# Decoding the weights of both layers inside the convolution stage, with operands in PSUM, and a three-pass filter transform

## The chip, the cores and the metric

One core of one Trainium2 chip runs the kernel. Its engines are TensorE (PE, matmuls; PEld is its weight load), VectorE (DVE), ScalarE (ACT), GpSimd (POOL) and the queues that issue DMAs (SP's and ACT's here). The metric is the device time of one execution in microseconds (us), the median of several.

## What is computed

A long convolution gates an input and is followed by two feed-forward layers. Cut to what matters:

```python
# x, v: (2, 12480, 128); filter from a small MLP times exp(-0.01 * pos)
h_filt = (np.maximum(pos_emb @ w1, 0.0) @ w2) * window
Uf = np.fft.rfft(x * v, n=2 * S, axis=1)
Hf = np.fft.rfft(h_filt, n=2 * S, axis=0)
y = np.fft.irfft(Uf * Hf[None], n=2 * S, axis=1)[:, :S]
a = (x * y).reshape(24960, 128)
h = a @ moe_w_in;  b = elu(h) @ moe_w_out           # 128 -> 2048 -> 128
h = b @ moe2_w_in; out = (h * np.cos(h)) @ moe2_w_out
```

The four weight matrices (128 x 2048 and 2048 x 128) reach the chip as 64-bit floats, so the kernel has to turn each into float32 with integer and float operations on its two 32-bit words. That is the decode. The layers multiply in fp32r, with each operand split into a high and a low part and three products in place of one float32 product, so the decode ends by splitting each weight into `hi` and `lo` too.

## The kernel before

**Stages.** The program is written by hand in one order for each engine: the engines take their instructions in the order of the Python code, and wait for each other by semaphores. A first stage (to some 50 us) makes the filter taps `h_all`. The second is the convolution, and then the two layers run over 52 tiles of 480 tokens each.

**The convolution** works on 32 groups of four channels (`NCH`, index `c`), in a software pipeline written as a table, `steps` (L424): each turn `p` of the loop at L427 runs each entry `(f, back, k)` for the group `p - back`. The stages are four small transforms. `st_a` (L330): PE multiplies by `fa_t` into `ps_a`, DVE makes `za` and `zb` by the twiddle factors, POOL adds them into `z_t`. `st_b` (L348): PE multiplies `z_t` by `dft_t` into `ps_b`. For `k == 2` this is the filter, and ACT copies the result to `hr` and `hi_f`. For `k` of 0 or 1 it is one of the two batches, and three DVE steps form the product with the filter (`ya`, `ps_b` in place, `y_t`); ACT rounds it to `yh`. `lo_y` (L326): POOL makes the rest `yl`. `st_c` (L376): PE transforms back into `ps_c`, in three fp32r passes, DVE makes `wa` and `wb`, POOL adds them into `w_t`. `st_d` (L401): PE makes `ps_d`, DVE multiplies by x into `at`, and SP's queue writes it to `xt_d` in DRAM. `prod` is POOL's product x * v (`u_t`), and `load` asks SP's queue for the next x and v. So a turn has three `st_a`, three `st_b`, two `st_c` and two `st_d`. `st_a` and `st_b` multiply in float32 (one such product is two PE instructions in the trace), `st_c` in fp32r.

**The decode of the first layer** is 16 jobs of 256 columns (`Decode`, L96). Between stages the loop takes one piece of it (`next(now)`, L432). On DVE it is `sg` and `mag` (sign and magnitude of the top word), `keep`, `bits`, `av` and `pw` (L119 to L141), all with operands in SBUF; on ACT `sq`, `lf` and `hi`; on POOL `bv`, `dv` and `lo`. SP's queue writes `hi` and `lo` to `w_d`.

**The layers.** Block `n` is a tile and one of eight groups of 256 hidden columns. `gemm1` (L496) makes `h_ps` with six fp32r matmuls of 480 columns; in layer 1, ACT's exponential and tanh and four DVE steps (L519, L521) make the activation; POOL or ACT and POOL split it (L93, L94); `gemm2` (L559) follows five blocks behind, with two of the eight groups in plain float32 (`gf`, eight PE instructions in a tile). After the last block of a tile ACT copies the result out (L578).

**The decode of the second layer** (`arena`, L592) is 8 jobs of 512 columns in free parts of `x1`. One piece of it stands behind each `gemm1` of the blocks 8 to 199 (L625). Here DVE does `dv` and `lo` as well (L161, L163, `self.e`).

Of the kernel before, what the change touches and what calls it, by code (L numbers as in the profile page):

```python
# [74 lines left out]
def hyena_moe_kernel(ctx: ExitStack, tc: tile.TileContext, x, v, pe, w1, w2,  # L75
# [20 lines left out]
    class Decode:  # L96


        def __init__(self, alloc, n, layer, which, q):
# [24 lines left out]

        def split(self):
            self.hi, self.lo = self.t("hi", F32R), self.t("lo", F32R)
            if not self.wide:
                self.av = self.raw
                copy_r(self.hi, self.raw)
                yield  # L130
                return
            keep, bits, self.av, pw, self.bv = (self.t("keep", I32), self.t("bits", I32), self.t("av", F32),
                                                self.t("pw", I32), self.t("bv", F32))
            nc.vector.tensor_scalar(keep, self.sq, TINY * TINY, -1.0, op0=ALU.is_ge, op1=ALU.mult)
            yield
            nc.vector.scalar_tensor_tensor(bits, self.mag, 0x40000000, self.sg,
                                           op0=ALU.bitwise_xor, op1=ALU.bitwise_or)
            yield
            nc.vector.tensor_tensor(self.av.bitcast(I32), bits, keep, op=ALU.bitwise_and)  # L139
            yield  # L140
            nc.vector.tensor_scalar(pw, self.av.bitcast(I32), -8388608, None, op0=ALU.bitwise_and)  # L141
            copy_r(self.hi, self.av)
            yield
            nc.gpsimd.tensor_tensor(self.bv, self.lf, pw.bitcast(F32), op=ALU.mult)
            yield

        def store(self):
            l, wh, n, p = self.layer, self.which, self.n, self.o
            nc.sync.dma_start(w_d[l, wh, 0, :, p:p + n], self.hi.bitcast(F32))
            for m in FULL[l] if wh else ():  # L150
                o = m * 256 - p
                if 0 <= o < n:
                    full = self.av[:, o:o + 256]
                    if self.wide:
                        full = self.t("full", F32)[:, 0:256]
                        nc.gpsimd.tensor_tensor(full, self.av[:, o:o + 256], self.bv[:, o:o + 256], op=ALU.add)
                        yield
                    nc.sync.dma_start(wf_d[l, m], full)
            if self.wide:
                dv = self.t("dv", F32)  # L160
                self.e.tensor_tensor(dv, self.av, self.hi.bitcast(F32), op=ALU.subtract)  # L161
                yield
                self.e.tensor_tensor(self.lo, dv, self.bv, op=ALU.add)  # L163
            else:
                nc.gpsimd.tensor_tensor(self.lo, self.av, self.hi.bitcast(F32), op=ALU.subtract)
            yield
            nc.sync.dma_start(w_d[l, wh, 1, :, p:p + n], self.lo.bitcast(F32))

        def run(self):
            for part in (self.words, self.split, self.store):  # L170
                yield from part()

    with tc.manual_schedule():
        with ExitStack() as cs:
# [132 lines left out]
            with ExitStack() as vs:  # L307
# [3 lines left out]
                pd = vs.enter_context(tc.tile_pool(name="pd", bufs=2, space=PSUM))  # L311
# [366 lines left out]
```

## Time and profile before

| | us |
|---|---|
| median of three runs | 3029.52 (3028.1 to 3030.63) |
| the profiled execution, its own time | 3032.04 |
| its span in the trace | 3030.2 |
| filter taps, first instruction to first `st_a` | 50.7 |
| convolution, first `st_a` to first `gemm1` | 689.5 |
| layer 1, first `gemm1` to its last copy-out (start) | 1169.5 |
| layer 2, from there to its last copy-out (start) | 1116.9 |

All stage times are differences of start times in the trace. The span is cut into these four by what PE does. Within a stage, the time from one occurrence of the same step to the next (one turn of the convolution's loop, one tile of a layer) tells more than the busy share of an engine over the span.

### The profile page before, as it was taken

The numbers are of one execution on the slowest core, as the hardware profiler recorded it, in microseconds if no ns is written. First come the engines' busy times: TensorE is split into PE (matmuls) and PEld (weight loads), VectorE is DVE, ScalarE is ACT, GpSimd is POOL, SyncE is SP. The second block draws the span as 40 slices with busy tenths as digits, with TensorE's granted clock in tenths as the row PEclk, the third lists the DMA queues.
The fourth block names the chain that finished last, engine by engine and source line by source line (L and its number), as shares of the span: only waits on it lengthen the run. The fifth ranks groups of instructions, "written<-read, shape, count | busy, mean of one in ns | idle before, by whom it ended". The sixth has DMA issues, their size and how long they took to land.

```text
span 3030.2 us, 38341 instructions
## 1 busy us (share of the span) xinstructions
PE 2966.4 (98%) x13140; PEld 2317.9 (76%) x13140; DVE 2587.9 (85%) x3272; ACT 2006.6 (66%) x3076; POOL 2575.1 (85%) x1632
## 2 busy tenths in 40 slices
PE   8999999998999999999999999999999999999999
PEld 6777677775777777888888887787888878888887
DVE  5999987876999998888888888788888888888887
ACT  2111111112887888888888888788888888888887
POOL 4888877775898998888888888888888888888888
PEclk9999999998999999999999999999999999999999
DMA  3232322222011100000000001000000000000000
GB/s 103 76 84 78 87 63 64 63 53 88 24 38 38 45 21 10 14 10 14 10 14 11 14 11 40 23 14 10 14 11 13 11 14 10 14 11 14 11 14 14
DMA packets 79635, 96.16 MB, mean 32 GB/s; under 512 B 5722, under 2 KB 63096, under 8 KB 79442
## 3 DMA queue, kind: packets, MB, share of 16 engines
q1 hardware_dynamic: 74016, 88.07, 10.0%
q10 hardware_dynamic: 5426, 5.65, 0.6%
q8 instruction: 105, 1.72, 0.2%
q14 instruction: 88, 0.72, 0.1%
HBM read 59.16 MB, written 34.54 MB: 31 GB/s over the span
## 4 chain that ended last, share of the span: by engine, by line
PE 83%; DVE 12%; issue 2%; ACT 2%; POOL 1%; DMA 0%; POOLq 0%; ACTq 0%; DVEq 0%
PE o_ps L573 34%; PE h_ps L504 32%; PE ps_b L356 6%; PE ps_c L387 4%; PE ps_d L405 2%; PE ps_a L336 2%; DVE e L519 2%; DVE e L521 2%; DVE wb L391 1%; DVE wa L391 1%; DVE ya L368 1%; DVE av L139 1%; ACT e L515 1%; DVE ps_b L369 1%; DVE zb L341 1%
## 5 line engine op out<-in xcount | busy, mean ns | idle before, releaser
L94 POOL TENSOR_TENSOR gl<-e,gh 128x960 fp32r<-128x960 f32 x624 | 1414.7, 2274 | 127.3 <-ACT gh L85 92.6
L504 PE MATMUL h_ps<-xh,w 128*128 128x480 f32 x3328 | 1074.8, 404 | 26.6 <-DVE e L521 22.6
L504 PEld LDWEIGHTS h_ps<-xh,w 128*128 128x128 f32 x3328 | 623.4, 188 | 220.6 <-issue 73.0
L573 PE MATMUL o_ps<-gh,w 128*128 128x480 f32 x2496 | 746.7, 380 | 0.0
L534 DVE SCALAR_TENSOR_TENSOR e<-e,h_ps 128x960 f32<-128x960 int32 x416 | 480.2, 1154 | 201.6 <-ACT e L532 146.9
L504 PE MATMUL h_ps<-xl,w 128*128 128x480 f32 x1664 | 632.8, 380 | 0.1
L519 DVE SCALAR_TENSOR_TENSOR e<-e,t_ps 128x480 f32<-128x480 f32 x832 | 534.4, 651 | 96.2 <-ACT t_ps L517 87.6
L515 ACT ACTIVATE e<-h_ps 128x480 f32<-128x480 f32 x832 | 473.0, 569 | 173.4 <-PE h_ps L504 143.7
L532 ACT ACTIVATE e<-h_ps 128x960 int32<-128x960 f32 x416 | 404.2, 972 | 200.0 <-PE h_ps L504 197.0
L573 PEld LDWEIGHTS o_ps<-gh,w 128*128 128x128 f32 x2496 | 468.9, 188 | 76.1 <-issue 0.8
L93 POOL TENSOR_SCALAR gh<-e 128x960 fp32r<-128x960 f32 x416 | 422.9, 1017 | 114.8 <-DVE e L521 88.9
L517 ACT ACTIVATE t_ps<-h_ps 128x480 f32<-128x480 f32 x832 | 476.4, 573 | 15.6 <-DVE e L519 15.5
L573 PE MATMUL o_ps<-gl,w 128*128 128x480 f32 x1248 | 476.4, 382 | 3.0 <-POOL gl L94 2.9
L541 ACT ACTIVATE e<-e,half_pi 128x960 f32<-128x960 f32 x416 | 453.6, 1090 | 0.3 <-DVE e L534 0.3
L521 DVE SCALAR_TENSOR_TENSOR e<-e,h_ps 128x480 f32<-128x480 f32 x624 | 377.6, 646 | 0.0
L573 PE MATMUL o_ps<-gf,wf 128*128 128x480 f32 x832 | 368.6, 565 | 0.0
L543 DVE TENSOR_TENSOR e<-e,h_ps 128x960 f32<-128x960 f32 x312 | 358.1, 1148 | 1.3 <-ACT e L541 1.2
L504 PEld LDWEIGHTS h_ps<-xl,w 128*128 128x128 f32 x1664 | 313.0, 188 | 53.3 <-POOL xl L94 0.8
L85 ACT ACTIVATE yh<-y_t 128x720 fp32r<-128x720 f32 x64 | 51.5, 805 | 411.2 <-DVE y_t L371 335.9
L573 PEld LDWEIGHTS o_ps<-gl,w 128*128 128x128 f32 x1248 | 234.7, 188 | 42.3 <-POOL gl L94 5.0
L356 PE MATMUL ps_b<-z_t,dft_t 128*128 128x360 f32 x768 | 254.3, 475 | 8.8 <-DVE y_t L371 8.2
L344 POOL TENSOR_TENSOR z_t<-za,zb 128x720 f32<-128x720 f32 x96 | 141.9, 1478 | 114.2 <-DVE zb L341 114.2
(94 smaller groups left out, 3479.0 us busy)
## 6 DMA issues: line engine op xcount, KB each, us to landing
x_t<-in_x SPq DMA_DIRECT2D x32, 392.0 KB
v_t<-in_v SPq DMA_DIRECT2D x32, 392.0 KB
xt_d<-at SPq DMA_DIRECT2D x64, 196.0 KB
out<-ot SPq DMA_DIRECT2D x52, 240.0 KB
x_in<-xt_d SPq DMA_DIRECT2D x50, 240.0 KB
w_d<-x SPq DMA_DIRECT2D x16, 256.0 KB
w<-w_d ACTq DMA_DIRECT2D x14, 256.0 KB
w<-w_d SPq DMA_DIRECT2D x14, 256.0 KB
```

Of the source, the lines that this page charges most:

```text
L93: ENG[plan[0]].tensor_scalar(hi, full, 1.0, 0.0, op0=ALU.mult, op1=ALU.add)
L94: ENG[plan[1]].tensor_tensor(lo, full, hi.bitcast(F32), op=ALU.subtract)
L356: nc.tensor.matmul(ps[:, r, 0:n], dft_t[:, sl], z[:, q], start=j == 0, stop=j == 1)
L504: nc.tensor.matmul(h[:, 0:T], a, b, start=k == 0, stop=k == 2)
L515: nc.scalar.activation(u[:, e], hs[e][:, 0:T], AF.Exp)
L517: nc.scalar.activation(ts[e][:, 0:T], hs[e][:, 0:T], AF.Tanh, scale=0.5)
L519: nc.vector.scalar_tensor_tensor(u[:, e], u[:, e], 1.0, ts[e][:, 0:T], op0=ALU.add, op1=ALU.mult)
L521: nc.vector.scalar_tensor_tensor(gt[:, e], u[:, e], 0.0, hs[e][:, 0:T], op0=ALU.min, op1=ALU.max)
L532: nc.scalar.activation(kq, hv, AF.Copy, scale=1.0 / TWO_PI, bias=0.25)
L534: nc.vector.scalar_tensor_tensor(rr, kq, -TWO_PI, hv, op0=ALU.mult, op1=ALU.add)
L541: nc.scalar.activation(rr, rr, AF.Sin, bias=half_pi)
L573: nc.tensor.matmul(o, a, b[:, e], start=f == 0 and k == 0, stop=f == NFT - 1 and k == len(mm) - 1)
```

## The change

All 32 jobs of both layers (256 columns each) are decoded in the convolution, and nothing of it is left in the layers. The decode is rewritten. ACT copies the top word into a PSUM tile `ps_w`, whose second half takes intermediate words, and does five more steps (`sq`, `keep` by Sign, `power`, `lf`, `hi`). DVE has four steps, `size`, `part`, `mag` and `pw`, each with at least one operand in `ps_w` and at most one in SBUF. POOL has three (`lf` times `pw`, `full`, `lo`). The pieces are taken by two generators, one for ACT's and DVE's part (`top`, four a turn) and one for POOL's (`low`, three a turn), which stand as entries in `steps`.

The filter's `st_b` (`k == 2`) becomes three fp32r passes, so `st_a` with `k == 2` gets a step of ACT (`zh`) and POOL one (`zl`, `lo_z`). `ps_d` has one bank in place of two, and the bank goes to `ps_w`. The table `steps` has another order: `st_b` of batch 0, `st_c` of batch 1 and `st_d` of batch 0 each come a turn later than before, and `load` comes at a turn's end.

```diff
+            sq, keep, power, size = self.t("sq", F32), self.t("keep", I32), self.t("power", I32), self.t("size", I32)
+            self.mag, self.lf, self.pw = self.t("mag", I32), self.t("lf", F32), self.t("pw", I32)
+            ps = bank.tile([128, 2, 256], F32, name="ps_w")
+            word, part = ps[:, 0].bitcast(I32), ps[:, 1].bitcast(I32)
+            nc.scalar.activation(ps[:, 0], top.bitcast(F32), AF.Copy)
+            nc.scalar.activation(sq, top.bitcast(F32), AF.Square)
             yield
+            nc.vector.tensor_scalar(size, word, 0x0FFFFFFF, 3, op0=ALU.bitwise_and, op1=ALU.logical_shift_left)
+            nc.scalar.activation(keep, sq, AF.Sign, scale=-1.0, bias=below)
+            yield
+            nc.vector.scalar_tensor_tensor(part, word, -2147483648, size, op0=ALU.bitwise_and, op1=ALU.bitwise_or)
+            nc.scalar.activation(power, keep, AF.Copy, scale=2.0 ** 23)
+            yield
+            nc.vector.scalar_tensor_tensor(self.mag, part, 0x40000000, keep, op0=ALU.bitwise_xor, op1=ALU.bitwise_and)
             nc.scalar.activation(self.lf, low.bitcast(U32), AF.Copy, scale=2.0 ** -52)
             yield
+            nc.vector.scalar_tensor_tensor(self.pw, part, 0x40000000, power, op0=ALU.bitwise_xor, op1=ALU.bitwise_and)
...
+                self.full = self.t("full", F32)
+                nc.gpsimd.tensor_tensor(self.lf, self.lf, self.pw.bitcast(F32), op=ALU.mult)
                 yield
+                nc.gpsimd.tensor_tensor(self.full, self.mag.bitcast(F32), self.lf, op=ALU.add)
+            hi, lo = self.t("hi", F32R), self.t("lo", F32R)
+            copy_r(hi, self.full)
             yield
+            nc.gpsimd.tensor_tensor(lo, self.full, hi.bitcast(F32), op=ALU.subtract)
+            nc.sync.dma_start(w_d[l, wh, 0, :, p:p + n], hi.bitcast(F32))
...
-                pd = vs.enter_context(tc.tile_pool(name="pd", bufs=2, space=PSUM))
+                pd = vs.enter_context(tc.tile_pool(name="pd", bufs=1, space=PSUM))
+                bank = vs.enter_context(tc.tile_pool(name="bank", bufs=1, space=PSUM))
...
+                    if k == 2:
+                        zh = p1.tile([NB, 2, DC * NF], F32R, name="zh")
+                        copy_r(zh, z)
+                        z = (z, zh)
                     zz[c, k] = z
+
+                def lo_z(c, k):
+                    z, zh = zz[c, k]
+                    zl = p1.tile([NB, 2, DC * NF], F32R, name="zl")
+                    nc.gpsimd.tensor_tensor(zl, z, zh.bitcast(F32), op=ALU.subtract)
+                    zz[c, k] = (zh, zl)
...
-                            nc.tensor.matmul(ps[:, r, 0:n], dft_t[:, sl], z[:, q], start=j == 0, stop=j == 1)
+                            if k == 2:
+                                zh, zl = z
+                                mm = ((dft_h, zh), (dft_l, zh), (dft_h, zl))
+                            else:
+                                mm = ((dft_t, z),)
...
-                steps = ((st_a, 0, 2), (st_b, 1, 1), (lo_y, 1, 0), (st_d, 2, 1), (prod, 0, 1), (st_a, 0, 0),
-                         (lo_y, 1, 1), (prod, -1, 0), (st_c, 1, 0), (st_b, 0, 2), (st_a, 0, 1),
-                         (st_c, 1, 1), (st_b, 0, 0), (st_d, 1, 0))
+                steps = ((st_b, 1, 0), (prod, 0, 1), (top, 0, 0), (lo_y, 1, 0), (low, 0, 0), (top, 0, 1), (st_a, 0, 2),
+                         (st_c, 2, 1), (top, 0, 2), (lo_z, 0, 2), (low, 0, 1), (st_b, 1, 1), (st_a, 0, 0), (lo_y, 1, 1),
+                         (st_d, 2, 0), (low, 0, 2), (st_c, 1, 0), (prod, -1, 0), (st_b, 0, 2), (st_a, 0, 1), (top, 0, 3),
+                         (st_d, 2, 1))
...
-        later = arena()
...
-                if 8 <= n < 200:
-                    next(later, None)
```

What POOL has in one turn of the convolution, before (one of the turns with decode; `bv`, `dv` and `lo` are its decode):

```order
L328 TENSOR_TENSOR yl_2319<-y_t_2276,yh_2278 128x720
L317 TENSOR_TENSOR u_t_2337<-x_t_1994,v_t_1995 98x512
L344 TENSOR_TENSOR z_t_2348<-za_2344,zb_2345 128x720
L328 TENSOR_TENSOR yl_2351<-y_t_2315,yh_2317 128x720
L317 TENSOR_TENSOR u_t_2354<-x_t_2175,v_t_2176 98x512
L398 TENSOR_TENSOR w_t_2389<-wa_2385,wb_2386 90x1024
L344 TENSOR_TENSOR z_t_2412<-za_2408,zb_2409 128x720
L144 TENSOR_TENSOR bv_2335<-lf_2302,pw_2334 128x256
L398 TENSOR_TENSOR w_t_2444<-wa_2440,wb_2441 90x1024
L161 TENSOR_TENSOR dv_2447<-av_2333,hi_2329 128x256
L163 TENSOR_TENSOR lo_2330<-dv_2447,bv_2335 128x256
L344 TENSOR_TENSOR z_t_2477<-za_2473,zb_2474 128x720
```

And in one turn of the change, from batch 0's `yl` on (the turn's first row, a `u_t`, is left off):

```order
L321 TENSOR_TENSOR yl_3186<-y_t_3178,yh_3180 128x720
L146 TENSOR_TENSOR lf_2962<-lf_2962,pw_2963 128x256
L337 TENSOR_TENSOR z_t_3202<-za_3198,zb_3199 128x720
L408 TENSOR_TENSOR w_t_3235<-wa_3231,wb_3232 90x1024
L348 TENSOR_TENSOR zl_3239<-z_t_3202,zh_3204 128x720
L148 TENSOR_TENSOR full_3189<-mag_2961,lf_2962 128x256
L337 TENSOR_TENSOR z_t_3266<-za_3262,zb_3263 128x720
L321 TENSOR_TENSOR yl_3268<-y_t_3253,yh_3255 128x720
L153 TENSOR_TENSOR lo_3243<-full_3189,hi_3242 128x256
L408 TENSOR_TENSOR w_t_3308<-wa_3304,wb_3305 90x1024
L310 TENSOR_TENSOR u_t_3310<-x_t_3166,v_t_3167 98x512
L337 TENSOR_TENSOR z_t_3339<-za_3335,zb_3336 128x720
```

A row more of the convolution (`zl`) is in each turn, the two `w_t` stand farther apart, and three decode rows are now in every turn, one by one between the others.

What DVE has in the convolution around its decode, before (`sg`, `mag`, `keep`, `bits`, `av`, and `pw` behind the second `wb`):

```order
L119 TENSOR_SCALAR sg_2303<-raw_2118 128x256
L368 TENSOR_TENSOR ya_2312<-ps_b_2307,hr_2217 128x720
L369 TENSOR_TENSOR ps_b_2307<-ps_b_2307,hi_f_2218 128x2x360
L371 TENSOR_TENSOR y_t_2315<-ya_2312,ps_b_2307 128x720
L122 TENSOR_SCALAR mag_2304<-raw_2118 128x256
L407 TENSOR_TENSOR at_2326<-ps_d_2323,x_t_1632 98x512
L134 TENSOR_SCALAR keep_2331<-sq_2301 128x256
L341 TENSOR_TENSOR za_2344<-ps_a_2339,tw_t_69 128x720
L341 TENSOR_TENSOR zb_2345<-ps_a_2339,tw_t_69 128x720
L136 SCALAR_TENSOR_TENSOR bits_2332<-mag_2304,sg_2303 128x256
L139 TENSOR_TENSOR av_2333<-bits_2332,keep_2331 128x256
```

And in the change, from the end of one turn into the next:

```order
L140 SCALAR_TENSOR_TENSOR pw_3736<-ps_w_3737,power_3732 128x256
L417 TENSOR_TENSOR at_3936<-ps_d_3933,x_t_3166 98x512
L378 TENSOR_TENSOR ya_3948<-ps_b_3943,hr_3904 128x720
L379 TENSOR_TENSOR ps_b_3943<-ps_b_3943,hi_f_3905 128x2x360
L381 TENSOR_TENSOR y_t_3951<-ya_3948,ps_b_3943 128x720
L129 TENSOR_SCALAR size_3926<-ps_w_3930 128x256
L133 SCALAR_TENSOR_TENSOR ps_w_3930<-ps_w_3930,size_3926 128x256
L334 TENSOR_TENSOR za_3971<-ps_a_3966,tw_t_74 128x720
L334 TENSOR_TENSOR zb_3972<-ps_a_3966,tw_t_74 128x720
L401 TENSOR_TENSOR wa_4004<-ps_c_3979,ti_t_75 90x1024
L401 TENSOR_TENSOR wb_4005<-ps_c_3979,ti_t_75 90x1024
L137 SCALAR_TENSOR_TENSOR mag_3927<-ps_w_3930,keep_3924 128x256
```

Six decode rows of a job have become four, all of them with `ps_w`, and `za`, `zb` of the filter come ahead of the `wa`, `wb` of the group before last.

In layer 1, DVE's rows before, over two blocks (`x1` to `x1` is the decode of the second layer):

```order
L519 SCALAR_TENSOR_TENSOR e2_7206<-e2_7206,t_ps_7217 128x480
L519 SCALAR_TENSOR_TENSOR e2_7206<-e2_7206,t_ps_7220 128x480
L521 SCALAR_TENSOR_TENSOR gf_7207<-e2_7206,h_ps_7208 128x480
L521 SCALAR_TENSOR_TENSOR gf_7207<-e2_7206,h_ps_7212 128x480
L139 TENSOR_TENSOR x1_5973<-x1_5973 128x512
L519 SCALAR_TENSOR_TENSOR e2_7237<-e2_7237,t_ps_7247 128x480
```

In the change the row of L139 and all others of that kind are gone there; nothing else stands otherwise in the layers.

## Rows read from the trace of the kernel before

**Rows 1.** The page: busy time, share of the span and instructions.
```profile
PE 2966.4 (98%) x13140; PEld 2317.9 (76%) x13140; DVE 2587.9 (85%) x3272; ACT 2006.6 (66%) x3076; POOL 2575.1 (85%) x1632
```

**Rows 2.** Engines by stretch: start and end, length, busy us and instructions of each.
```profile
195.00:279.90 84.90, 81.78 (x418) 60.58 (x417) 78.64 (x97) 15.49 (x32) 70.18 (x49) 1.00 0.30 82
512.60:593.60 81.00, 81.00 (x417) 60.74 (x416) 64.66 (x73) 11.22 (x20) 60.08 (x37) 1.00 0.23 60
781.00:1086.00 305.00, 288.02 (x1192) 219.97 (x1191) 300.63 (x479) 247.87 (x477) 272.75 (x165) 1.00 0.12 38
1110.00:1410.00 300.00, 300.00 (x1283) 240.37 (x1282) 267.51 (x447) 252.06 (x488) 268.33 (x168) 1.00 0.05 12
```

**Rows 3.** Timeline of PE, one turn without decode: start us, duration us, line, instructions.
```profile
553.13 1.39 PE L336 MATMUL ps_a<-fa_t,h_all 98*128 98x180 f32 x8
554.50 2.66 PE L356 MATMUL ps_b<-z_t,dft_t 128*128 128x360 f32 x8
556.99 1.88 PE L405 MATMUL ps_d<-w_t,g_t 90*98 90x512 f32 x4
558.71 1.39 PE L336 MATMUL ps_a<-fa_t,u_t 98*128 98x180 f32 x8
...
562.76 2.58 PE L356 MATMUL ps_b<-z_t,dft_t 128*128 128x360 f32 x8
...
565.18 1.39 PE L336 MATMUL ps_a<-fa_t,u_t 98*128 98x180 f32 x8
...
573.37 0.93 PE L336 MATMUL ps_a<-fa_t,h_all 98*128 98x180 f32 x5
```

**Rows 4.** Timeline of PE: first turn's start, last turn's start, drain, first gemm1.
```profile
66.37 0.93 PE L336 MATMUL ps_a<-fa_t,h_all 98*128 98x180 f32 x5
...
694.81 1.39 PE L336 MATMUL ps_a<-fa_t,h_all 98*128 98x180 f32 x8
...
730.08 1.96 PE L405 MATMUL ps_d<-w_t,g_t 90*98 90x512 f32 x4 [0.63 <-POOL w_t L395]
734.34 3.73 PE L405 MATMUL ps_d<-w_t,g_t 90*98 90x512 f32 x4 [2.31 <-POOL w_t L395]
740.19 1.17 PE L504 MATMUL h_ps<-xh,w 128*128 128x480 f32 x2 [2.12 <-POOL xh L93]
```

**Rows 5.** Timeline of ACT, copy-outs of layer 1's tiles 1, 14 and 28.
```profile
780.26 0.58 ACT L578 ACTIVATE x<-o_ps 128x480 f32<-128x480 f32 x1
...
1086.13 0.57 ACT L578 ACTIVATE x<-o_ps 128x480 f32<-128x480 f32 x1
...
1387.70 0.57 ACT L578 ACTIVATE x<-o_ps 128x480 f32<-128x480 f32 x1
```

**Rows 6.** Groups by line, 781 to 1086 us: count, busy us, mean ns, idle before.
```profile
L504 PE MATMUL h_ps<-xh,w 128*128 128x480 f32 x413 | 132.1, 400 | 15.9 <-DVE e L521 14.7 <-DVE gf L521 1.1
```

**Rows 7.** Groups by line in the convolution, 75 to 700 us: count, busy us, mean ns.
```profile
L328 POOL TENSOR_TENSOR yl<-y_t,yh 128x720 fp32r<-128x720 f32 x60 | 105.6, 1760 | 0.0
L341 DVE TENSOR_TENSOR za<-ps_a,tw_t 128x720 f32<-128x720 f32 x90 | 80.8, 898 | 18.1 <-POOL u_t L317 16.8 <-PE ps_a L336 1.3
L356 PEld LDWEIGHTS ps_b<-z_t,dft_t 128*128 128x128 f32 x720 | 129.8, 189 | 72.8 <-POOL w_t L398 6.2 <-issue 5.7
L85 ACT ACTIVATE yh<-y_t 128x720 fp32r<-128x720 f32 x60 | 48.3, 805 | 386.0 <-DVE y_t L371 315.4 <-POOL yl L328 65.9 <-PE ps_a L336 4.7
L139 DVE TENSOR_TENSOR av<-bits,keep 128x256 int32<-128x256 int32 x16 | 25.3, 1583 | 1.1
L136 DVE SCALAR_TENSOR_TENSOR bits<-mag,sg 128x256 int32<-128x256 int32 x16 | 7.9, 494 | 0.0
L144 POOL TENSOR_TENSOR bv<-lf,pw 128x256 f32<-128x256 f32 x16 | 11.7, 730 | 0.0
L118 ACT ACTIVATE sq<-raw 128x256 f32<-128x256 f32 x15 | 6.4, 425 | 0.0
```

**Rows 8.** The group of L136 in 195 to 279.9 us, four turns with decode.
```profile
L136 DVE SCALAR_TENSOR_TENSOR bits<-mag,sg 128x256 int32<-128x256 int32 x4 | 1.6, 408 | 0.0
```

More of the change, by code (lines that the diff above doesn't have):

```diff
@@ L110, in __init__, with bits @@
                                   w[o:o + n, :].rearrange("(k p) d -> p k d", p=128))
-        def words(self):
+        def bits(self):
             if not self.wide:
+                self.full = self.raw
+                yield
                 return
@@ L135, in split @@
             yield
[L136 to L144, printed above, removed]
@@ L152, in store @@
                 if 0 <= o < n:
[L153 to L165, printed above, removed]
+                    nc.sync.dma_start(wf_d[l, m], self.full[:, o:o + 256])
             yield
[L167 to L171, printed above, removed]
+            nc.sync.dma_start(w_d[l, wh, 1, :, p:p + n], lo.bitcast(F32))
+    one = ctx.enter_context(tc.tile_pool(name="one", bufs=1))
+    below = one.tile([128, 1], F32, name="below")
     with tc.manual_schedule():
+        nc.vector.memset(below, BELOW)
         with ExitStack() as cs:
@@ L355, in st_b @@
                         for j, (sl, q) in enumerate(prs[r]):
-                            nc.tensor.matmul(ps[:, r, 0:n], dft_t[:, sl], z[:, q], start=j == 0, stop=j == 1)
+                            if k == 2:
[3 more added lines that the diff above has]
+                                mm = ((dft_t, z),)
+                            for i, (a, b) in enumerate(mm):
+                                nc.tensor.matmul(ps[:, r, 0:n], a[:, sl], b[:, q], start=j == 0 and i == 0,
+                                                 stop=j == 1 and i == len(mm) - 1)
                     if k == 2:
@@ L410, in alloc, with bits_of_all @@
                 def alloc(name, dt):
-                    return (p2 if name == "raw" else p1).tile([128, 256], dt, name=name, tag=f"d_{name}")
-                def first_layer():
-                    jobs = [(0, w, q) for w in range(2) for q in range(DFF // 256)]
+                    return (p1 if name in ("sq", "keep", "power", "size") else p2).tile([128, 256], dt, name=name, tag=f"d_{name}")
+                jobs = [(l, w, q) for l in range(2) for w in range(2) for q in range(DFF // 256)]
+                ready = []
+                def bits_of_all():
                     nxt = Decode(alloc, 256, *jobs[0])
@@ L587, in reload @@
                 layers[1].load(nc.sync, wh, m)
-        ARENA = T * 20
-        ASIZE = (B * S - ARENA) // 2
-        def arena():
-            jobs = [(1, w, q) for w in range(2) for q in range(DFF // 512)]
-            for i, job in enumerate(jobs):
-                free = [ARENA + i % 2 * ASIZE]
-                def alloc(name, dt):
-                    n = 512 * (2 if name == "raw" and dt != F32 else 1)
-                    t = x1[:, free[0]:free[0] + n]
-                    free[0] += n
-                    return t if dt == F32 else t.bitcast(dt)
-                dec = Decode(alloc, 512, *job)
-                for _ in range(4):
-                    yield
-                yield from dec.run()
-        later = arena()
         for wh in range(2):
```

49 lines of the change are left out of this document (24 added, 25 removed).

## Prediction, made before the changed kernel ran

> **What bounds the kernel now.** I read the page's busy line first, then the engines by stretch, then PE's timeline inside one turn and one tile. PE is busy for 98% of the span [rows 1], so time can only go where PE has less to do or where it waits. The stretches show where it waits. In four turns of the convolution without decode (512.6 to 593.6) PE is busy for 81.0 of 81.0 us; in four with decode (195.0 to 279.9) for 81.8 of 84.9, and there DVE is at 78.6. In layer 1 with decode (781 to 1086) PE has 288.0 of 305 us and DVE 300.6, in layer 1 without it (1110 to 1410) PE has 300 of 300 and DVE 267.5 [rows 2]. So wherever a weight is decoded DVE sets the pace, and elsewhere PE does. Layer 2 has no decode and nothing of the change.
>
> **The sizes.** A turn without decode takes 573.37 - 553.13 = 20.24 us, and there PE never pauses: `st_a` 1.37 (553.13 to 554.50), float32 `st_b` 2.42 to 2.49 (562.76 to 565.18, 554.50 to 556.99), `st_d` 1.72 (556.99 to 558.71), `st_a` with `st_c` 4.05 (558.71 to 562.76), so `st_c` 2.68 or 0.112 a matmul of 256 columns [rows 3]. The real mean is longer: the thirty turns from 66.37 to 694.81 take 20.95 each [rows 4]. A tile of layer 1 with decode takes (1086.13 - 780.26) / 13 = 23.53 us, one without (1387.70 - 1086.13) / 14 = 21.54 [rows 5].
>
> **Part 1, layer 1 without decode.** The 13 tiles fall from 23.53 to 21.54: 25.8 us. PE's wait for DVE's `e` is 15.9 us of this in the matmuls' own rows [rows 6]; the rest is wait that the weight loads take first. What is late next is PE itself, busy for 300 of 300 us once the decode is over [rows 2]. The first tile is filling its pipeline, with no decode yet to lose. I take 25.
>
> **Part 2, the three-pass filter `st_b`.** Eight float32 instructions of 0.303 (2.42 / 8) become twelve fp32r of 360 columns. A tile's 21.54 us are 84 fp32r matmuls and eight float32 instructions of 480 columns; with the latter at 0.303 x 480 / 360 = 0.403, an fp32r one is (21.54 - 3.23) / 84 = 0.218. Between 0.112 for 256 columns and 0.218 for 480, 360 columns give 0.161, so 12 x 0.161 = 1.94. That saves 0.48 a turn. The bounds: if each pass waited for its weight load (189 ns [rows 7]) it would be 2.27 and save 0.15; but `st_a` loads as many weights and goes at 1.37 / 8 = 0.17 a load, so I keep 1.94. PE's floor for a turn is then 20.24 - 0.48 = 19.76.
>
> **Part 3, does a turn with a whole decode job fit in 19.76?** Sums first, on four turns without decode [rows 2]. DVE: 64.66 / 4 = 16.2, plus four decode steps. The trace shows none with a PSUM operand; the cheapest row like them, `bits` among four quiet turns, is 0.408 [rows 8], the dearest is `av` at 1.583 [rows 7]. `av` reads two operands from SBUF, the new steps at most one. DVE rows with one SBUF and one PSUM operand do not stretch: `za` is 0.898 over all turns [rows 7]. I take 0.41, so 17.8; the dear end would be 22.5. POOL: 60.08 / 4 = 15.0, plus `zl` at the 1.76 of `yl` and three decode steps at 0.73 [rows 7]: 19.0, or 19.3 with POOL's convolution rows as long as in the turns with decode. ACT: 11.22 / 4 = 2.8, plus `zh` 0.8 and six steps of 0.42 [rows 7]: 6.1. So PE stays the longest, with POOL at 96 to 98% of it.
>
> On the dear end the Trainium skill has a rule (SBUF — State Buffer, section Who interferes with whom): a DVE instruction with at most one SBUF input, outside its two-port modes, does not contend with GpSimd, and one with two SBUF inputs does. By it the sum is 17.8, by `av` 22.5; `za` agrees with it, and no row here has integer words in PSUM.
>
> Then the order. I put PE's ten stages end to end from `st_b` of batch 0 (time 0) and let each other engine take its rows in order, 0.2 after their source. DVE: `y` of batch 0 ends at 5.3, `size` and `part` 6.1, filter's `zb` 7.8, `wb` of batch 1 10.1, `mag` 10.5, `y` of batch 1 13.1, `zb` 14.8, `at` 15.4, `wb` of batch 0 17.7, last `zb` 19.9, `pw` 20.3, `at` 20.9; the next turn's `ya` can start at 22.4. POOL: `yl` starts at 6.2 (after ACT's `yh`), then `lf` 8.6, filter's `z` 10.1, `w` 12.7, `zl` 14.4, `full` 15.1, `z` 16.6, `yl` 18.3, `lo` 19.0, `w` 21.4, `u` 22.7, `z` 24.2, `u` 25.5; its next `yl` is ready at 25.95. So POOL runs some 4 us into the next turn and has 0.45 to spare.
>
> The waits that the change adds fit into this walk. The filter's `st_b` starts on PE at 14.75 and wants `zl` for its third matmul at 15.1, ready at 14.4: 0.7 spare, and behind it on PE stand `st_a` and `st_d`. `st_d` with one bank wants `at` from 15.4 at 18.0. ACT's copy into `ps_w` waits for `pw` at 20.3; behind it stand `sq` and `yh`, whose `y` comes at 25.0. ACT's `hi` waits for `full` at 15.1, and behind it `yh` of batch 1 ends at 16.4, just before POOL wants it at 16.6; this is the tightest place. SP's queue gets three more DMAs a turn than without decode, but about as many as it has in the early turns.
>
> With so little to spare I add 0.2 a turn: 19.95. From the first `st_a` of turn 1 to `gemm1` is now 740.19 - 66.37 = 673.8 [rows 4]. In the change turn 1 lacks a `st_c` and two `st_d` and has some waits of the fill, 15.3; 29 turns at 19.95 are 578.6; the drain from the last turn's `st_a`, walked in the same way, is 44.6 where it was 45.4. Its end is the same chain, last `st_d`, DMA, first `gemm1` (10.1 from 730.08 [rows 4]). Sum 638.5, a gain of 35. At 19.76 it is 41. The fill before 66.37 has the same order on PE, with `zh` and `zl` under a wait for `h_all` and `ps_a`: nothing.
>
> **Sum.** 25 + 35 = 60. The profiled execution took 3032.0 and its span is 3030.2; 3032.0 - 60 = 2972. The median of the runs is 2.5 lower, so 2969.5, rounded to 2969.
>
> **The rivals.**
> A, the forecast: 2960 (no wait in the convolution) to 2980.
> B, POOL is the bound. Its 19.3 and five waits of 0.2 to 0.3 a turn (for DVE's `zb` and `wb` and ACT's `yh`) make 20.4 to 20.8; with the middle, 20.6, 29 x 0.65 = 19 us more: 2988. For it: POOL is at 96% by the sum, and one late row moves all behind it. Against it: the walk has it done 0.45 before its next row is ready.
> C, slower: DVE's decode steps wait for POOL as `av` does, 1.583 each although one operand is in PSUM. A turn is then 22.5, 29 x 2.55 = 74 us more: 3043. It decides from 22.0 a turn, where the 60 us are used up, or 1.45 a step. For it: `bits` is 0.494 over all turns against 0.408 in quiet ones, and each DVE decode row of layer 1 is stretched. Against it: `za`.
> D, layer 1 does not get its 25 us back, because its early tiles wait for something else than the decode (their x from DRAM, say): 2994. Against it: DVE is at 300.6 of 305 there.
>
> **How the numbers follow.** A 0.65, B 0.23, D 0.05, C 0.07. The range takes in A, the weight-load bound of part 2 (9 us, inside A) and most of B: 2958 to 2992. This measurement can tell about 0.2% (6 us) from no change. A, B and D are faster; C is slower at its full price and about level if a step takes 1.4 to 1.5. So faster 0.93, same 0.02, slower 0.05.
>
> **What the new profile would show.** Right: thirteen more tiles of 21.5 in layer 1 with PE busy throughout; turns of 19.8 to 20.1; fp32r `ps_b` matmuls some 0.16 apart; `size`, `part`, `mag`, `pw` at about 0.4; POOL busy for 19 of each turn with short waits. B: PE waiting for POOL's `zl`, `yl` or `w_t`, with POOL busy without a gap. C: these four rows above 1 us and DVE full. What would make it wrong most easily is the place where ACT's `hi` holds `yh`: a late POOL row comes back to POOL by it.

## The result, and the profile after

The changed kernel takes 2959.58 us (median of four runs, 2956.26 to 2961.15); the kernel before takes 3030.07 us on the same chip. The ratio is 0.9766, with a 95% interval of 0.9749 to 0.9783: 70.5 us faster, where 60 were forecast. The profiled execution has a span of 2959.4 us.

The page's busy line and its chain of waits, changed kernel:

```profile
PE 2930.0 (99%) x13268; PEld 2336.0 (79%) x13268; DVE 2508.3 (85%) x3241; ACT 2073.8 (70%) x3228; POOL 2629.2 (89%) x1700
PE 97%; POOL 1%; DVE 1%; issue 1%; ACT 0%; DMA 0%; ACTq 0%; POOLq 0%; DVEq 0%
```

Against [rows 1], POOL and ACT have more to do and PE 36 us less, and the chain runs through PE almost alone. The same by stretch (start and end, length, busy time of PE, PEld, DVE, ACT and POOL, then the granted clock). The first row is four turns of the convolution, each with a whole decode job; the second is 306 us of layer 1:

```profile
358.74:437.02 78.28, 78.28 (x434) 62.63 (x433) 69.17 (x88) 23.39 (x48) 75.09 (x53) 1.00 0.33 89
736.00:1042.00 306.00, 306.00 (x1309) 245.53 (x1309) 273.23 (x456) 257.89 (x498) 273.11 (x173) 1.00 0.05 13
```

A turn takes 78.28 / 4 = 19.57, where the kernel before needs 21.2 with decode and 20.24 without [rows 2, 3]. The trace gives PE no pause in either stretch. Per turn DVE has 17.3, ACT 5.85 and POOL 18.8. The turns from PE's timeline (start, duration, line, tiles; the first `st_a` of turns 1, 3 and 31, and the first `gemm1`):

```profile
68.12 1.08 PE L329 MATMUL ps_a<-fa_t,h_all 98*128 98x180 f32 x6
...
104.31 0.78 PE L329 MATMUL ps_a<-fa_t,h_all 98*128 98x180 f32 x4
...
652.30 0.93 PE L329 MATMUL ps_a<-fa_t,h_all 98*128 98x180 f32 x5
...
697.74 1.17 PE L533 MATMUL h_ps<-xh,w 128*128 128x480 f32 x2 [2.67 <-POOL xh L95]
```

The 28 turns from 104.31 to 652.30 take 19.57 each (the one before them, from 84.29, still takes 20.02). From turn 1 to `gemm1` it is 629.6, where it was 673.8 [rows 4]: 44.2 less. Turn 1 starts 1.75 later than before. In layer 1, ACT's copy-outs of the first, the fourteenth and the last tile:

```profile
736.90 0.57 ACT L607 ACTIVATE x<-o_ps 128x480 f32<-128x480 f32 x1
...
1016.93 0.57 ACT L607 ACTIVATE x<-o_ps 128x480 f32<-128x480 f32 x1
...
1838.97 0.56 ACT L607 ACTIVATE x<-o_ps 128x480 f32<-128x480 f32 x1
```

Thirteen tiles take 280.03, or 21.54 each, where they took 23.53 [rows 5]: 25.8 less. The spans of the two profiled executions differ by 70.8 us: 42.4 up to the first `gemm1`, 25.8 in these tiles, 0.9 in the first tile (40.07 to 39.16) and 1.55 in the last of layer 1 (26.46 to 24.91). Layer 2 is as long as before, 1116.9.

### The profile page after: what moved, and what is told of

It reads as the page before. It is cut to its first block, busy times and chain, and to the rows that moved or that the text cites. A ratio compares the mean times of both kernels' runs of the same rounds, so it can differ in the third digit from the quotient of the medians.

```text
span 2959.4 us, 38859 instructions
## 1 busy us (share of the span) xinstructions
PE 2930.0 (99%) x13268; PEld 2336.0 (79%) x13268; DVE 2508.3 (85%) x3241; ACT 2073.8 (70%) x3228; POOL 2629.2 (89%) x1700
## 4 chain that ended last, share of the span: by engine, by line
PE 97%; POOL 1%; DVE 1%; issue 1%; ACT 0%; DMA 0%; ACTq 0%; POOLq 0%; DVEq 0%
PE o_ps L602 39%; PE h_ps L533 37%; PE ps_b L365 7%; PE ps_c L397 6%; PE ps_a L329 4%; PE ps_d L415 3%; PE h_ps L266 1%; PE w_ps L207 0%; PE r_ps L248 0%; POOL z_t L337 0%; POOL yl L321 0%; DMA wf<-wf_d 0%; POOL u_t L310 0%; POOL zl L348 0%; POOL w_t L408 0%
## 5 line engine op out<-in xcount | busy, mean ns | idle before, releaser
L533 PEld LDWEIGHTS h_ps<-xh,w 128*128 128x128 f32 x3328 | 626.3, 188 | 192.4 <-issue 70.8
L548 DVE SCALAR_TENSOR_TENSOR e<-e,t_ps 128x480 f32<-128x480 f32 x832 | 543.3, 654 | 121.6 <-ACT t_ps L546 109.5
L95 POOL TENSOR_SCALAR gh<-e 128x960 fp32r<-128x960 f32 x416 | 416.1, 1000 | 115.8 <-DVE e L550 95.5
L602 PEld LDWEIGHTS o_ps<-gf,wf 128*128 128x128 f32 x832 | 157.0, 189 | 100.8 <-issue 88.6
L87 ACT ACTIVATE gh<-e 128x960 fp32r<-128x960 f32 x208 | 208.0, 1000 | 11.1 <-PE o_ps L602 11.1
L365 PE MATMUL ps_b<-z_t,dft_t 128*128 128x360 f32 x512 | 165.9, 466 | 1.9 <-DVE y_t L381 1.7
```

The source lines that it names most:

```text
L95: ENG[plan[0]].tensor_scalar(hi, full, 1.0, 0.0, op0=ALU.mult, op1=ALU.add)
L365: nc.tensor.matmul(ps[:, r, 0:n], a[:, sl], b[:, q], start=j == 0 and i == 0, stop=j == 1 and i == len(mm) - 1)
L533: nc.tensor.matmul(h[:, 0:T], a, b, start=k == 0, stop=k == 2)
L548: nc.vector.scalar_tensor_tensor(u[:, e], u[:, e], 1.0, ts[e][:, 0:T], op0=ALU.add, op1=ALU.mult)
L602: nc.tensor.matmul(o, a, b[:, e], start=f == 0 and k == 0, stop=f == NFT - 1 and k == len(mm) - 1)
```

## The experiments

Each ratio is against the kernel before on the same chip, which took 3026.2 to 3027.4 us there (medians).

### What each part is worth

**Layer 1 without its decode, in the kernel before.**

```diff
-                    q.dma_start(t, wf_d[self.l, m])
+                    q.dma_start(t, wf_d[0, m])
...
-                if 8 <= n < 200:
-                    next(later, None)
```

> The kernel before without the second layer's decode in layer 1; layer 2 uses layer 1's weights, so its values differ. Theory: what layer 1 gained in the change is all of it the absent decode: the 13 tiles fall to 21.54 (25.8 us), the first tile by 0.9 and the last by 1.5 us; the time is 3030 - 28 = 3002. Rival: part of the 28 us came from something else in the change (where the convolution ends, how the two stages meet), and the first or the last tile stays as it was: 3004.

3000.81 us, ratio 0.9915 (0.9900 to 0.9929), 25.6 us faster. ACT's copy-outs of the first and the fourteenth tile:

```profile
776.70 0.57 ACT L578 ACTIVATE x<-o_ps 128x480 f32<-128x480 f32 x1
...
1056.73 0.58 ACT L578 ACTIVATE x<-o_ps 128x480 f32<-128x480 f32 x1
```

21.54 a tile, as in the changed kernel. The first tile (40.25) and the last (26.47) stay as they were, so these are not the decode's; in this the theory fell and the rival is right.

**The changed kernel with the decode of one layer only.**

```diff
-                jobs = [(l, w, q) for l in range(2) for w in range(2) for q in range(DFF // 256)]
+                jobs = [(l, w, q) for l in range(1) for w in range(2) for q in range(DFF // 256)]
```

> The changed kernel with the 16 jobs of the first layer's weights alone; layer 2 uses layer 1's weights, so its values differ. Turns from 18 on have no decode on any engine. Theory: the decode costs nothing in its new place; turns are 19.57 in both halves, and the time is 2960 within 3. Rival: POOL or DVE sets the turn in part; the later turns fall below 19.57 (to 19.4 or less), and the time to 2957 or less.

2959.12 us, ratio 0.9776 (0.9761 to 0.9790). Turns are 19.57 in the half with decode (104.18 to 358.61, 13 turns) and in the half without (358.61 to 652.18, 15 turns). In its new place the decode costs the turns nothing.

**The changed kernel with the filter's `st_b` in float32.** `zh`, `zl` and the passes are gone; order and decode stay.

```diff
-                            if k == 2:
-                                zh, zl = z
-                                mm = ((dft_h, zh), (dft_l, zh), (dft_h, zl))
-                            else:
-                                mm = ((dft_t, z),)
+                            mm = ((dft_t, z),)
```

> The changed kernel with the filter's st_b back in float32 (no zh, zl, lo_z); the rest stays. Theory: PE alone sets the turns, and the 0.22 us a turn by which the turns without decode before (20.24) lie above the bare sum of their stages was a wait for ps_b's bank that the new order of stages removed. Then a turn is 19.57 + 0.45 = 20.02 us and the time 2959.6 + 32 x 0.45 = 2974. Rival: the three passes gave more than 0.45 and the order gave nothing, so that a turn goes back to 20.24 and the time to 2981.

2968.35 us, ratio 0.9808 (0.9793 to 0.9822). The turn is the theory's, the rival's 20.24 is out. The first `st_a` of turns 3 and 31:

```profile
101.99 1.39 PE L329 MATMUL ps_a<-fa_t,h_all 98*128 98x180 f32 x8
...
662.18 1.39 PE L329 MATMUL ps_a<-fa_t,h_all 98*128 98x180 f32 x8
```

28 turns of 20.01. The passes are worth 0.44 a turn, and the other 0.23 against the 20.24 of before come from elsewhere: with PE doing the same work, the turn is shorter, so the kernel before waits in turns whose PE reads as always busy. Where, the section on the prediction shows.

### Why the decode fits: operands in PSUM

```diff
-            ps = bank.tile([128, 2, 256], F32, name="ps_w")
+            ps = p1.tile([128, 2, 256], F32, name="ps_w", tag="d_psw")
```

> The changed kernel with ps_w, the tile of the top words, in SBUF in place of PSUM; the same instructions in the same order. Theory: part, mag and pw now read two operands from SBUF and wait for POOL as av did before (1.58 us), so that DVE needs 16.2 + 0.4 + 3 x 1.2 to 1.6 = 20.2 to 21.4 us a turn, turns are 20.3 to 21.5, and the time is 2980 to 3020. Rival: it is the smaller number of steps and not their place that made the decode cheap; each step stays at 0.41, a turn at 19.57, the time at 2960.

3061.48 us, ratio 1.0114 (1.0099 to 1.0129); turns of 23.14 on average. DVE's decode rows by line, 200 to 400 us (busy us, mean ns):

```profile
L140 DVE SCALAR_TENSOR_TENSOR pw<-ps_w,power 128x256 int32<-128x256 int32 x9 | 38.1, 4233 | 0.0
...
L137 DVE SCALAR_TENSOR_TENSOR mag<-ps_w,keep 128x256 int32<-128x256 int32 x9 | 6.6, 731 | 0.0
L133 DVE SCALAR_TENSOR_TENSOR ps_w<-ps_w,size 128x256 int32<-128x256 int32 x9 | 3.8, 425 | 0.3
```

and the same three lines in the changed kernel, 358.74 to 437.02:

```profile
L133 DVE SCALAR_TENSOR_TENSOR ps_w<-ps_w,size 128x256 int32<-128x256 int32 x4 | 1.7, 432 | 0.1
...
L140 DVE SCALAR_TENSOR_TENSOR pw<-ps_w,power 128x256 int32<-128x256 int32 x4 | 1.7, 415 | 0.0
L137 DVE SCALAR_TENSOR_TENSOR mag<-ps_w,keep 128x256 int32<-128x256 int32 x4 | 1.6, 410 | 0.0
```

The same instruction takes 4233 ns with both operands in SBUF and 415 with one in PSUM. The direction is the theory's, the size is beyond its upper end of 3020: `pw` stands in a stretch where POOL's rows follow each other without a gap. One `pw` runs from 405.32 to 411.27, 5.95 us, and POOL has four rows in a line from 404.64 to 410.98. `part` (L133) also has two SBUF operands and does not stretch: it comes while POOL waits for ACT's `yh`, as at 391.19, where POOL is idle from 389.99 to 391.87. So what POOL does at that moment decides, and not the instruction alone. The Trainium skill (SBUF — State Buffer, section Who interferes with whom) says that a DVE instruction with two SBUF inputs contends with a GpSimd instruction that reads SBUF, and that one with at most one SBUF input, outside the two-port modes, does not. The trace agrees for `pw`, and for the four steps of the change; the old decode's `sg` and `mag` have one SBUF input and do wait (below), and no run here shows whether they ran in such a mode.

### Why the decode fits: the order of stages

**The old order, with all else of the change** (two lines of the table; the `top`, `low` and `lo_z` entries spread over it).

```diff
+                steps = ((st_a, 0, 2), (top, 0, 0), (st_b, 1, 1), (lo_y, 1, 0), (low, 0, 0), (st_d, 2, 1), (top, 0, 1),
+                         (prod, 0, 1), (lo_z, 0, 2), (st_a, 0, 0), (lo_y, 1, 1), (low, 0, 1), (prod, -1, 0),
...
```

> The changed kernel with the stages in the order of before, the decode's pieces and lo_z set between them. Theory: the order is worth only the wait for ps_b's bank, 0.22 us a turn: 19.8, time 2967. Rival: with POOL at 96% of a turn the decode fits only in the new order; PE then waits for POOL's zl, yl or w_t, turns are 20.5 or more and the time above 2988.

3034.84 us, ratio 1.0030 (1.0019 to 1.0042); turns of 22.07. The theory fell: 19.8 was expected of PE's sums. POOL's timeline, then DVE's (a wait and its releaser in brackets):

```profile
277.47 1.73 POOL L321 TENSOR_TENSOR yl<-y_t,yh 128x720 fp32r<-128x720 f32 x1
279.15 0.75 POOL L148 TENSOR_TENSOR full<-mag,lf 128x256 f32<-128x256 f32 x1
279.86 1.33 POOL L310 TENSOR_TENSOR u_t<-x_t,v_t 98x512 f32<-98x512 f32 x1
281.13 2.43 POOL L408 TENSOR_TENSOR w_t<-wa,wb 90x1024 f32<-90x1024 f32 x1
```

```profile
283.59 1.22 DVE L401 TENSOR_TENSOR wa<-ps_c,ti_t 90x1024 f32<-90x1024 f32 x1 [2.49 <-POOL w_t L408]
```

`wa` has one buffer. The second `st_c` of a turn writes it again, and so waits until POOL's `w_t` has read it; `w_t` stands behind `yl`, `full` and `u_t`. DVE, which holds the next stages, loses 2.49 there. The rival's size came, but not by the waits that it named: PE's longest is for DVE, at the `st_b` that wants the bank `ps_b` (150 to 640 us: total, times, longest):

```profile
PE ps_b L365 <- DVE y_t L381: 33.0, 22, 1.6
```

**The same with two buffers for `wa` and `wb`.**

```diff
-                    t1 = p1.tile([NF, DC * n], F32, name="wa")
-                    t2 = p1.tile([NF, DC * n], F32, name="wb")
+                    t1 = p2.tile([NF, DC * n], F32, name="wa")
+                    t2 = p2.tile([NF, DC * n], F32, name="wb")
```

> As e3_old_order (old order, the rest of the change), but with two buffers each for wa and wb, so that wa of batch 1 need not wait for POOL's w_t of batch 0. Theory: that wait closes the loop in e3_old_order; without it wa starts when st_c ends, 1.5 us earlier, and a turn is 20.2 to 20.7, the time 2984 to 2998. Rival: POOL's order as such sets the turn, and its w_t is as late as before; a turn stays above 21.5 and the time above 3020.

2989.43 us, ratio 0.9877 (0.9863 to 0.9892); turns of 20.58. As the theory had it: this wait was 1.5 of the 2.5 a turn. Of the rest, a row by line (250 to 450 us, the last field is idle time and its releaser):

```profile
L337 POOL TENSOR_TENSOR z_t<-za,zb 128x720 f32<-128x720 f32 x30 | 44.6, 1487 | 18.9 <-DVE zb L334 18.9
```

POOL waits 1.9 a turn for DVE, and with 18.8 of work has no such room within 20. What the other 1.0 of the old order would need was not tested further.

**The old order with the new decode, filter in float32** (the table above without `lo_z`, and the edit of `st_b` above).

> The changed kernel with the old order of stages (as e3_old_order) and the filter's st_b in float32 (no zh, zl, lo_z). In e3_old_order, whose turns took 21.95, DVE's wa of batch 1 waited 2.5 us for POOL's w_t of batch 0, and POOL was late there by its rows since the turn's start. Theory: zl, 1.74 us of POOL ahead of that w_t, is what the old order cannot take; without it turns are 20.2 to 20.6 and the time 2980 to 2992. Rival: the old order cannot take the decode's POOL rows either; turns stay at 21.3 or more, the time at 3014 or more.

3000.02 us, ratio 0.9913 (0.9898 to 0.9928); turns of 21.02, between theory and rival. Without `zl` a turn is 1.05 of the 2.5 shorter, though PE has 0.45 more to do.

**The new order alone, on the kernel before** (its table without `top`, `low` and `lo_z`).

> The kernel before with the new order of stages alone (old decode, float32 filter, second layer decoded in layer 1). Theory: turns without decode fall from 20.24 to 20.02, since st_b of batch 1 no longer waits for y_t; turns with decode stay near 21.2, where DVE's 21 us of rows set the pace. Time 3026 - 3 = 3023. Rival: the order also takes away the waits of the turns with decode; these fall to 20.6 or less, time 3012 or less.

3048.80 us, ratio 1.0067 (1.0050 to 1.0084). Turns without decode take 20.01 (495.74 to 715.82, 11 turns), as the theory had it: that is the 0.23 again, with the old decode and without the passes. Turns with decode take 24.5, against 21.2 in the old order, where 21.2 or less was expected. DVE by line, 220 to 400 us:

```profile
L119 DVE TENSOR_SCALAR sg<-raw 128x256 int32<-128x256 int32 x7 | 17.4, 2482 | 0.0
L122 DVE TENSOR_SCALAR mag<-raw 128x256 int32<-128x256 int32 x7 | 17.3, 2473 | 0.0
```

The old decode's rows meet POOL rows that now follow each other more closely: the `mag` from 259.16 to 263.47 ends just behind POOL rows that stand without a gap longer than 0.1 from 251.73 to 263.31. These two steps have one SBUF input only, so two inputs are not the only case in which a DVE step waits beside POOL.

**The three passes alone, on the kernel before** (`lo_z` behind `prod` of batch 1).

```diff
+                        zh = p1.tile([NB, 2, DC * NF], F32R, name="zh")
+                        copy_r(zh, z)
...
+                    nc.gpsimd.tensor_tensor(zl, z, zh.bitcast(F32), op=ALU.subtract)
```

> The kernel before with the three-pass filter st_b alone (zh, zl and lo_z too), order and decode as they were. Theory: in the turns with decode DVE sets the pace, so that PE's 0.45 us gain nothing there; the 12 turns without decode gain 0.45 each: 6 us, time 3024. Rival: PE's saving counts in each of the 32 turns: 14 us, time 3016.

3082.36 us, ratio 1.0182 (1.0167 to 1.0197). Both expectations fell. Nine turns with decode, then eleven without:

```profile
141.94:364.25 222.31, 198.41 (x974) 155.66 (x973) 194.26 (x217) 41.30 (x81) 173.62 (x118) 0.92 0.25 71
527.85:750.68 222.83, 217.85 (x1189) 171.96 (x1188) 176.66 (x199) 39.74 (x66) 184.11 (x111) 1.00 0.21 57
```

Without decode a turn takes 20.26: PE has 0.45 less to do and waits 0.45 more, all of it at one place, `st_b` of batch 1. In PE's timeline:

```profile
570.18 2.66 PE L372 MATMUL ps_b<-z_t,dft_t 128*128 128x360 f32 x8 [0.45 <-DVE y_t L388]
```

So in the old order it is this wait for DVE's `y_t`, which still reads the bank `ps_b`, that sets the turn, and not PE's work. With decode a turn takes 24.7, with DVE's `keep` at 1951 ns and PE idle for a tenth; the granted clock is 0.92 there. Why `keep` is so long was not tested.

So the parts do not add up: the order alone costs 0.7% and the passes alone 1.8%, but the whole change gains 2.3%, of which layer 1 without its decode is 0.85%.

### How much room POOL has

```diff
+                def more(c, k):
+                    nc.gpsimd.tensor_tensor(pad[:, 0], pad[:, 0], pad[:, 1], op=ALU.add)
```

> The changed kernel with two more POOL additions of 128x256 in every turn (on a tile of zeros that nothing else reads, values unchanged). Theory: POOL has 19.57 - 18.8 = 0.8 us a turn to spare; with 1.46 more it is the bound, a turn is 20.2 to 20.3 and the time 2979. Rival: POOL has more room than its busy time says, since its rows overlap and its waits give way; a turn stays at 19.6 to 19.8, the time at 2960 to 2966.

2974.55 us, ratio 0.9828 (0.9812 to 0.9844); turns of 20.07. Four of them (columns as above):

```profile
367.12:447.46 80.34, 79.42 (x433) 62.60 (x432) 69.17 (x88) 23.37 (x48) 80.34 (x61) 1.00 0.32 87
```

POOL is busy for 80.34 of 80.34, and the theory is right but for 0.15 a turn: POOL's rows overlap a little (their durations add up to 82.3). It is the bound as soon as a turn gives it 1.5 more, so the change leaves it some 0.8 a turn, and its busy share can be believed here: a turn is as long as its rows.

### The joint of convolution and layer 1

Over these kernels the first tile of layer 1 took 34.5 to 40.3 us, with no relation to the edits. The changed kernel was run with 36 idle matmuls in PE's last gaps of the convolution, beside itself.

```diff
+                        if p == NCH + 1 and f is st_d:
+                            keep_busy(12 if k == 0 else 24)
```

> The changed kernel with 36 fp32r matmuls of 256 columns added at the end of the convolution, whose results nobody reads: 12 behind the st_d of batch 0 of the last group and 24 behind the last st_d. In the changed kernel the granted clock between 692 and 712 us is 0.52, the last st_d takes 3.73 us where others take 1.72 to 1.88, and the first tile of layer 1 takes 39.2 us; over the kernels of this study that tile took between 34.5 and 40.3, and where it was 34.5 the clock of this stretch was 0.76. Theory: the clock falls because TensorE waits between the last steps of the convolution, and this costs the first tile; with the matmuls in these gaps the clock stays above 0.7, the last st_d takes about 1.9, the first tile 34.5 to 36, and the time is 3 to 5 us below the changed kernel of the same call (about 2955). Rival: the wait for the first x of layer 1 lowers the clock whatever stands before it, and the added matmuls (36 of 0.11 us, 4 us, partly in front of the first gemm1) give nothing or cost up to 4 us.

> The changed kernel itself, again, as the measure for the run beside it: 2956 to 2961 us, a ratio of 0.975 to 0.978, turns of 19.57, and a first tile of layer 1 of 39.2 us if its length belongs to the program, anywhere between 34.5 and 40.3 if it differs from one execution to the next.

2956.39 us (2955.53 to 2956.63, four runs) with the matmuls, 2957.59 (2954.70 to 2960.85, five runs) without; ratios 0.9768 (0.9755 to 0.9781) and 0.9772 (0.9759 to 0.9786). The last `st_d` with the matmuls, and then without:

```profile
690.47 1.96 PE L415 MATMUL ps_d<-w_t,g_t 90*98 90x512 f32 x4 [1.19 <-POOL w_t L405]
```

```profile
690.62 3.73 PE L415 MATMUL ps_d<-w_t,g_t 90*98 90x512 f32 x4 [2.63 <-POOL w_t L405]
```

and the stretch around it, in the same order (the granted clock is the third field from the end, a mean of its two levels: 1.00 is 2.4 GHz, 0.50 is 1.2):

```profile
692.00:712.00 20.00, 14.88 (x62) 10.97 (x61) 11.83 (x22) 11.29 (x23) 8.06 (x7) 0.86 0.44 141
```

```profile
692.00:712.00 20.00, 14.64 (x33) 8.81 (x31) 8.99 (x16) 9.31 (x19) 5.98 (x5) 0.55 0.44 141
```

The clock is as the theory had it: over the 20 us from 5 before `gemm1` it is 0.85 with the matmuls and 0.54 to 0.78 in all kernels without them. `st_d` takes 1.96 in place of 3.73. That the first tile gains by it is not shown. It took 35.7 in place of 37.9, but it was as short without the matmuls in the kernels with the words in SBUF and with the old order in float32 (34.6 and 34.5), and in the kernel with two more POOL additions the last `st_d` took 1.96 and the first tile 36.3. In time the rival's "nothing" fits: the median falls by 1.2 us, not 3 to 5, and that is less than these runs can tell. `gemm1` comes 46.1 after the last turn's start with the matmuls, 45.1 and 45.4 without.

The runs with the matmuls lie within 1.1 us, those without within 6.2; but the kernel with half the decode, without the matmuls, lay within 0.6, so this is not shown to be their work either. The changed kernel's first tile was 39.2 in one profile and 37.9 in another, so its length belongs to the execution. The last tile of layer 1 does too: 24.9 in the first profile of the changed kernel, 26.45 in the second. PE pauses there about as long in both (busy for 8.17 and 8.29 of 10 us), but the clock is 1.00 in the first and 0.83 in the second:

```profile
1820.00:1830.00 10.00, 8.17 (x35) 6.14 (x34) 5.58 (x9) 4.70 (x7) 8.03 (x5) 1.00 0.31 96
```

```profile
1820.00:1830.00 10.00, 8.29 (x31) 7.10 (x32) 3.77 (x5) 3.49 (x4) 5.70 (x4) 0.83 0.19 55
```

## Why the prediction was right, and where it was off

**The number: in the range, and in part by luck.** 2959.58 is 1.6 above the lower end of the range, and below the 2960 that the prediction gave for no wait at all. Two errors in the convolution stand against each other: the turns took 10.6 us less than forecast, the fill and the drain 3.4 more. Without the second error the time would have been about 2956, below the range.

**Layer 1: right.** 25 forecast, 25.8 measured, and 25.6 with this part alone. Rival D is out. One row is misread without effect: 15.9 is all the idle time in [rows 6], of which 14.7 is for `e`.

**The size of the passes: right.** Twelve at 0.164 (1.97 in all) against 0.161. The small difference comes from `st_c`: taken with a `st_a` that was too long (below), it came to 2.68, where it is 2.83 or 0.118 a matmul. By 0.118 the same working gives 0.164.

**DVE's decode steps: right.** 0.410 to 0.432 against 0.41. DVE's sum is 17.3 (17.8), POOL's 18.8 (19.0), ACT's 5.85 (6.1). Rival C's mechanism is real and was taken away by PSUM: with the words in SBUF a turn takes 23.1, near the 22.5 that it gave. It comes about otherwise, though: by one step at 4.23 and not by four at 1.58.

**PE's floor: the step that failed.** The prediction read "there PE never pauses" from [rows 2, 3] and took 20.24 as PE's work, from which the passes' 0.48 could be taken. In the old order they shorten no turn without decode (20.26). The changed kernel has the same stages with their bare lengths, in PE's timeline:

```profile
421.50 2.58 PE L365 MATMUL ps_b<-z_t,dft_t 128*128 128x360 f32 x8
423.92 1.39 PE L329 MATMUL ps_a<-fa_t,u_t 98*128 98x180 f32 x8
425.14 0.59 PE L415 MATMUL ps_d<-w_t,g_t 90*98 90x512 f32 x1
...
429.68 0.33 PE L365 MATMUL ps_b<-zh,dft_h 128*128 128x360 f32 x1
...
431.65 1.39 PE L329 MATMUL ps_a<-fa_t,u_t 98*128 98x180 f32 x8
432.88 0.59 PE L415 MATMUL ps_d<-w_t,g_t 90*98 90x512 f32 x1
434.60 0.47 PE L365 MATMUL ps_b<-z_t,dft_t 128*128 128x360 f32 x1
```

From start to start, `st_a` takes 1.22 (with `st_d` behind it), float32 `st_b` 2.42, the passes 1.97, `st_d` 1.72. In [rows 3] the first `st_a` lasts 1.37 and the `st_b` behind it 2.49: 0.15 and 0.07 too long. That `st_b` starts at 554.50 because its bank `ps_b` is still being read by DVE; the page's durations are modelled and run into the wait (1.39 is given for `st_a` whether the next starts 1.22 or 1.37 later), so no idle time appears. DVE's row in the kernel before:

```profile
553.44 0.91 DVE L371 TENSOR_TENSOR y_t<-ya,ps_b 128x720 f32<-128x720 f32 x1
```

It ends at 554.35. The Trainium skill (Perfetto Trace Analysis, section Tensor Engine Instruction (MATMUL, LD_WEIGHTS)) says that the profiler estimates a matmul's end and does not observe it; the trace agrees. The three passes in the old order show the same wait in the open: there `st_b` starts 1.83 after its `st_a`, and the profile names `y_t`. The bare sum is 20.02, less 0.45 for the passes 19.57: exactly the turn. The new order puts `st_a` and `st_c` between batch 0's `st_b` and batch 1's, where `st_d` and `st_a` stood, and the 0.22 are gone, in the float32 version of the change and in the new order alone alike.

**The 0.2 added for waits: not needed.** In a turn of the change neither the trace nor a stage longer than its shortest shows a wait of PE, and a turn with no decode in it is as long (19.57). Together with the floor this is 578.6 - 568.0 = 10.6 us for 29 turns, the whole of the miss and more. Rival B is out: POOL's only wait is `yl` of batch 0 for `yh`. The place called tightest, ACT's `hi` that holds `yh` of batch 1, is as the walk had it. ACT's timeline, then POOL's:

```profile
430.01 0.42 ACT L87 ACTIVATE hi<-full 128x256 fp32r<-128x256 f32 x1 [3.70 <-POOL full L148]
430.33 0.79 ACT L87 ACTIVATE yh<-y_t 128x720 fp32r<-128x720 f32 x1
```

```profile
421.31 1.72 POOL L321 TENSOR_TENSOR yl<-y_t,yh 128x720 fp32r<-128x720 f32 x1 [0.82 <-ACT yh L87]
...
431.37 1.74 POOL L321 TENSOR_TENSOR yl<-y_t,yh 128x720 fp32r<-128x720 f32 x1
```

`yh` ends at 431.12 and POOL comes at 431.37: 0.25 to spare, where 0.2 were reckoned. At the turn's end POOL waits 0.82, where 0.45 were.

**Fill and drain: off the other way.** Turn 1 is 16.17 (15.3 forecast), the drain 45.4 (44.6), and turn 1 starts 1.75 later, where nothing was set. That gives back 3.4. In the fill's trace DVE's first `size` stands before `za` and waits 2.2 for ACT's copy of the first weights, and PE's first three-pass `st_b` waits 0.74 for `zl`. How much of the 1.75 is theirs stays open: from the first `st_a` to turn 1 it is 17.0 and 16.75 in two profiles of the changed kernel, 15.7 in the kernel before, but 14.0 in that kernel without the second layer's decode, whose convolution is the same. With 10.6 on the other side the convolution gains 42.4 in place of 35. So the 10.5 us that were missed are 7.2 here, 0.8 in layer 1's thirteen tiles and 2.5 at the two joints. The 2.5 us at the two joints can't be put down to the change, since these tiles differ by as much between executions of one kernel.

**Where the convolution's gain lies.** The 29 turns from turn 2 on took 606.0 and take 568.0, 38.0 less. By difference, with 29 turns each, 13 of it are the passes (0.44 a turn) and 7 the wait for `ps_b` (0.23); the other 18 are the turns with decode, which took 21.1 to 22.2 and are now as long as the rest.

## What to carry to other kernels

PE at 100% busy is not PE at its floor: compare the same stage's start-to-start time at several places of the loop, with an eye on what stands behind it (a `st_a` before `st_c` reads 1.10 here, and that `st_c` is longer by as much). A stage that is longer somewhere may hide a wait, and a new order can get it back. A second test is to give PE less work: where the turn stays as long, PE did not set it. The decode on DVE beside a busy POOL was cheap here with one operand of each step in PSUM, and then the order of stages decided whether it fits. Parts of such a change may each lose alone, so an edit tried by itself says little about the whole.

## What the runs showed of the hardware

A DVE step of 128 x 256 integers with both operands in SBUF took 4.23 us on average (200 to 400 us) and 6.25 at most in that run, longer than POOL's longest row in that stage (2.63): it can wait through several POOL rows that follow each other. The old decode's `sg` and `mag`, each with a single SBUF input, took 2.48 beside denser POOL rows, up to 5.24. So the 0.408 of a quiet row [rows 8] is no guide for rows on SBUF beside a busy POOL. With an operand in PSUM none of the four stretched, at POOL 96% busy: all 32 jobs took 0.41 to 0.43 a step. In a quiet place PSUM is the slower of the two for a step with one input: `size` took 0.42 from PSUM and 0.285 from SBUF.

At the joints of stages two executions of the changed kernel had a granted clock of 0.52 and 0.55 beside a first tile of 39.2 and 37.9 us, and of 1.00 and 0.83 beside a last tile of 24.9 and 26.45.
